# Attention maxima in two-bank PSUM tiles, one VectorE reduction per step, blocks of two row pairs

## The chip, the core and the metric

The kernel runs on one core of a Trainium2 chip. The metric is the device time of one launch in microseconds (us); of several runs the median is taken. A core has TensorE (PE in the profile; its weight loads are PEld), VectorE (DVE), ScalarE (ACT), GpSimd (POOL) and SyncE (SP), which issues most DMAs. PSUM holds eight banks of 512 fp32 values for each of 128 partitions; a matmul writes into one bank.

## The reference, cut to what matters

One block of a transformer with a conditioned layer norm: attention with 32 heads of 16 over 2048 tokens of 512 features, and after it a token-mixing and a channel MLP. The change touches attention alone:

```
q, k, v = split(h @ wqkv)                        # 32 heads of 16, S = 2048
scores  = einsum("bhqd,bhkd->bhqk", q, k) * 16**-0.5
p       = softmax(scores, axis=-1)
x       = x + ga * ((p @ v) @ wo)
```

The kernel takes the maximum of each row of scores before the exponential, so it computes the scores twice: once with queries on the partitions, for the row maxima, and later with keys on the partitions, for the exponentials that go into the product with v.

## The kernel before

**Units and steps.** Attention is cut into 64 units: 4 chunks of 512 queries (`ci`), in each 16 pairs of heads (`pr`). The two heads of a pair, `j` = 0 and 1, lie on partitions 0 to 63 and 64 to 127 of the tiles `qtl` (queries) and `kst` (keys). A unit has 16 steps, one for each tile of 128 keys, 1024 steps in all (`NS`). A step `s` has two *row pairs*, one for each `j`. A row pair (`row_pair`) issues two matmuls of 512 columns that lie on different halves of TensorE's rows: one of the scores of step `s` (`score_part`, L1012, tile `sc`) and one of the scores of step `s + 24` (`LEAD`) for the maxima (`max_part`, L996, tile `mb`). Where the score is that of `j`, the maximum is that of `1 - j`, and the matmul on rows 0 to 63 is issued first.

**Who empties the banks.** ScalarE turns each score bank into exponentials (L1008, `pt<-sc`, 128x512); VectorE reduces each maxima bank to one column (L992, `mx<-mb`, 128x512 to 128x1). When a unit's 32 reductions are through, `max_fin` reduces the columns to 8 maxima (L1042), two ScalarE copies and one GpSimd operation split them into two parts, and DMAs put them into spare rows of `qtl`, so that the score matmul subtracts them.

**The second half of a probability.** An exponential is kept as two 16-bit halves. The low halves of a step (128x1024) must be converted once (`p_low`). GpSimd does it (L1061); where the planner holds GpSimd to be over 200 ns further behind than ScalarE (`LACT`), ScalarE does it (L156, the line of a helper).

**Column parts.** `pv_part` issues four matmuls of 32 columns at a time into the single `pv` bank (L1086 for the high halves of a step, L1083 for the low halves of two). A pair of steps has three such parts. At a unit's end ScalarE copies `pv` out (`ac`, L1103), TensorE transposes the copy with eight matmuls (`ot`, L1113), ScalarE copies these (L1120), VectorE takes reciprocals (L1128) and GpSimd multiplies.

**Banks.** `pv` has one bank. The other seven are slots of one bank each (`NSM`, class `Slots`), and whoever asks next, a score, a maxima tile or `ot`, takes the slot that comes free first.

**The order.** All instructions are emitted by a planner on the host (`Sched`), which keeps an expected time for each engine (605 ns for a reduction, 480 for an exponential, 232 for a row pair, 240 for a column part) and so fixes each engine's order; on the chip semaphores decide when each starts. The main loop goes by *blocks*: `GRP` = 3 row pairs, that is one step and a half, and then the column parts of steps that lie `LAG` = 2 blocks back. The first 256 steps share TensorE with leftover projections; steps 256 to 993 have attention, nearly alone; in the last 30 (`T0S`) the next stage begins.

```
def room(self, n=1):
    if self.slots:
        return self.open is None and len(self.owner) < self.most and min(self.slots.t) <= self.T["P"]
blocks = [list(range(i, min(i + GRP, 2 * NS))) for i in range(-2 * LEAD, 2 * NS, GRP)]
```

Of the kernel before, what the change touches and what calls it, by code (L numbers as in the profile page):

```python
# [8 lines left out]
F32 = mybir.dt.float32  # L9
# [5 lines left out]
AF = mybir.ActivationFunctionType  # L15
OP = mybir.AluOpType
AX = mybir.AxisListType
# [4 lines left out]
P = 128  # L22
# [31 lines left out]
LENDS = -4  # L54
LATE = 1e9
GRP = 3
CPER = 1
LACT = 200.0
PRE = 1
# [52 lines left out]
class Sched:  # L112
# [163 lines left out]
    def room(self, n=1):  # L276

        if self.slots:
            return self.open is None and len(self.owner) < self.most and min(self.slots.t) <= self.T["P"]
        for x in [x for x in self.back if x[1] <= self.T["P"]]:  # L280
            self.back.remove(x)
            self.avail.append(x[0])
        return len(self.avail) >= n
# [21 lines left out]
class Slots:  # L305


    def __init__(self, n):
        self.t = [0.0] * n

    def take(self):
        return min(range(len(self.t)), key=lambda i: self.t[i])

    def late(self):
        return sum(t == LATE for t in self.t)
# [15 lines left out]
def kernel(ctx, tc, A_x, A_wqkv, A_wo, B_w1, B_w2, B_w3, B_w4, c, w_mod, out):  # L331
# [622 lines left out]
    psd["d"], psd["s"] = ap_, True  # L954

    unit_tiles(at, 1, pool, pool)
    qst, vst, mxs = {}, {}, {}
# [15 lines left out]
    sm = Slots(NSM)  # L973
    e_exp, e_hi, e_low, v_free, acs = {}, {}, {}, [0.0], []

    def bank(nm):
        x = sm.take()
        return x, ap_.tile([P, CH], F32, name=nm, tag=f"s{x}", bufs=1)

    def max_part(m, j):  # L980

        u, i = divmod(m, 16)
        c, g = divmod(i, 4)
        if u not in mxs:
            mxs[u] = at.tile([P, 2, 4, NC], F32, name="mx", tag="mx", bufs=2)
        x, b = bank("mb")
        ready, sm.t[x] = sm.t[x], LATE
        r = slice(64 * j, 64 * j + 62)
        lhs = qst[u][r, (g // 2) * 256:(g // 2 + 1) * 256].rearrange("p (n l) -> p l n", l=2)[:, g % 2]

        def after(e):
            end = sch.crit("D", 605, e + PX, lambda: dve.reduce_max(mxs[u][:, j, g, c:c + 1], b, axis=AX.X))  # L992
            sm.t[x] = end + XP["D"]
            if (c, g, j) == (NC - 1, 3, 0):
                max_fin(u)
        return ready, lambda: te.matmul(b, lhs, kst[u % 3][r, c * CH:(c + 1) * CH], start=True, stop=True), after  # L996

    def score_part(s, j):

        u, kt = divmod(s, NKT)  # L1000
        if j == 0:
            pt[s] = at.tile([P, 2, CH], I32, name="pt", tag="pt", bufs=NPT)
        x, b = bank("sc")
        ready, sm.t[x] = sm.t[x], LATE
        r = slice(64 * j, 64 * j + 64)

        def after(e):
            ea = sch.crit("A", 480, e + PX, lambda: act.activation(pt[s][:, j], b, AF.Exp))  # L1008
            sm.t[x] = ea + XP["A"]
            if j:  # L1010
                e_exp[s] = e_hi[s] = ea
        return ready, lambda: te.matmul(b, kst[u % 3][r, kt * P:(kt + 1) * P], qst[u][r], start=True, stop=True), after  # L1012

    def row_pair(s, j):

        parts = []
        if 0 <= s < NS:
            parts.append((j, score_part(s, j)))
        if s + LEAD < NS:
            parts.append((1 - j, max_part(s + LEAD, 1 - j)))  # L1020
        parts = [x for _, x in sorted(parts, key=lambda x: x[0])]

        def mms():
            for _, mm, _ in parts:
                mm()
        e = sch.put("P", CROW, max(x[0] for x in parts), mms)
        return [partial(x[2], e) for x in parts]

    def max_fin(u):
        mf = at.tile([P, 8], F32, name="mf", tag="mf", bufs=2)  # L1030
        nm = at.tile([P, 2, 8], F32R, name="nm", tag="nm", bufs=2)
        mx = mxs.pop(u)

        def shift_rows():
            for j in range(2):
                for i in range(2):
                    r = 64 * j + 62 + i
                    for h in range(2):
                        sch.dma(dma.dma_start,
                                qst[u][r:r + 1, h * 256:(h + 1) * 256].bitcast(F32).rearrange("o (p l) -> o p l", l=2),  # L1040
                                nm[:, i, 4 * j + 2 * h:4 * j + 2 * h + 2].bitcast(F32))
        sch.chain(("D", 85, lambda: dve.reduce_max(mf.rearrange("p (j g) -> p j g", j=2), mx, axis=AX.X)),  # L1042
                  ("A", 100, lambda: act.activation(mf, mf, AF.Copy, scale=-1.0, bias=PEXP)),
                  ("A", 100, lambda: act.activation(nm[:, 0], mf, AF.Copy)),
                  ("G", 250, lambda: pool.tensor_tensor(nm[:, 1], mf, nm[:, 0], op=OP.subtract)),
                  (None, 0, shift_rows), mark(("shift", u)), prio=0, ready=sch.T["D"])
# [549 lines left out]

    blocks = [list(range(i, min(i + GRP, 2 * NS))) for i in range(-2 * LEAD, 2 * NS, GRP)]
    pvs = [x for s in range(0, NS, 2) for x in ((s, 0), (s + 1, 0), (s, 1))]  # L1600
    due = 0.0
    for k, blk in enumerate(blocks + [[]] * (LAG + CPER)):
        if blk and blk[0] <= LENDS <= blk[-1]:
            sch.most = MOST
        for x in blk:
            if x % 2 == 0:
                if x == blk[0]:
                    before(x // 2)
                if x >= 0 and x % 32 == 0:
                    drain(("shift", x // 32))  # L1610
        if acs:
            ac_copy()
        row = [divmod(x, 2) for x in blk if x < 2 * NS]
        s0 = row[0][0] if row else 0
        col = []
        if k >= LAG and (k % CPER == 0 or not blk):

            x = (blocks[min(k - LAG, len(blocks) - 1)] or [-1])[-1]
# [3 lines left out]
        need = sum((s >= 0) + (s + LEAD < NS) for s, _ in row)  # L1622
        sch.flush(need)
        banks = sorted(sm.t)
        n = 0
        for s, i in row:
            n += (s >= 0) + (s + LEAD < NS)

            start = max(start, banks[n - 1 + 2 * (s < 0)] - t)
            t += CROW  # L1630
        t += CMID
        for s, i in col:
            start = max(start, pv_ready(s, i) - t)
            t += CCOL
        sch.gap(start)
        sch.flush(need)
        sch.T["P"] = max(sch.T["P"], start) + CIN
        low = sorted(e_exp)
        for s, i in row:
            for fn in row_pair(s, i):  # L1640
                fn()
        for x in blk[1:]:
            if x % 2 == 0:
                before(x // 2)
        for s in low:
            p_low(s)
        sch.T["P"] += CMID
        for s, i in col:
            pv_part(s, i)
        sch.T["P"] += COUT  # L1650
        for e in "ADG":
            sch.misc(e, max(sch.T["P"], sch.T[e]) + TOLE[e])
        if s0 < 0:
            sch.fill(LEADB / 2 * len(blk))
        elif sch.gens:
            late = s0 >= NS - T0S
            due += RATE3 if late else RATE if s0 < NS // NC else RATE2
            if due >= (BURST3 if late else BURST if s0 < NS // NC else BURST2):
                sch.fill(due)
                due = 0.0  # L1660
        if 2 * (NS // NC) - 1 in blk:
            for key in (("v", 1), ("kq", 3), ("q", 0), ("q", 1), "pieces"):
                drain(key)
            qpx.close()
            sch.gapmin = GAPMIN2
            ot = o0x.enter_context(tc.tile_pool(name="ot", bufs=1, side="right"))
            for ci in range(1, NC):
                oh[ci] = ot
                osb[ci] = ot.tile([P, TPC, D], F32, name=f"osb{ci}", tag=f"osb{ci}", bufs=1)
            fa = o0x.enter_context(tc.tile_pool(name="fa", bufs=1, side="right"))  # L1670
            big = {"A4": fa.tile([P, 4 * KT * 2 * P], F32R, name="A")}
            big["A"] = big["A4"]
        if blk and blk[0] <= 2 * (NS - T0L) <= blk[-1]:
            sch.add(tail_loads())
        if blk and blk[0] <= 2 * (NS - T0S) <= blk[-1]:
            sch.add(tail(0))
    if acs:
# [3 lines left out]
    sch.most = 0  # L1681
    while sch.owner:
        sch.step()
    apx.close()
    sch.banks(8)
    with ExitStack() as ex:
# [44 lines left out]
```

## Time and profile before

| what | value |
|---|---|
| median of 3 runs | 2022.87 us (2017.93 to 2027.44) |
| profiled execution | span of 2019.7 us; the runs' median is 3.2 us above |
| busy over the span | PE 96%, DVE 82%, ACT 75%, POOL 78% |
| granted TensorE clock | 0.992 mean |

How to read it: the span is from the first to the last instruction of one profiled execution. A busy share is an average over stages with different limits; the page therefore shows each engine in 40 slices of the span, and a view by windows gives the busy time of each engine in one stretch. The groups by line give count, busy time and the mean duration of one instruction. A duration reaches from an instruction's start to the acknowledgement of its last write, while the next instruction of VectorE or ScalarE may start some 80 ns before that; so the distance between neighbours is read from a row of the timeline that merges many of them. "Idle before" is time in which the engine waited, with the instruction that released it. Matmuls on different row or column groups of TensorE run side by side, so a step of TensorE is read from the starts of neighbouring groups, not from its busy share.

### The profile page before, as it was taken

Reading aid. Unit: us, or ns where it says so; the run is one execution under the profiler, and the core shown is the slowest. Engines: PE = TensorE matmul, PEld = TensorE weight load, DVE = VectorE, ACT = ScalarE, POOL = GpSimd, SP = SyncE. Lnnn points to the kernel's source line nnn. Section 1 sums busy time; section 2 is a strip of 40 time slices with the busy share of each in tenths; the row PEclk is TensorE's granted clock in tenths of the full one; section 3 lists DMA queues with packets and bytes.
Section 4 is the critical chain, followed back from the end, with each engine's and each line's share of the span. In section 5 each row is a group of like instructions: output and inputs, shape, how many; then the busy total and the mean of one; then the engine's idle time right before and its main releaser. Section 6 shows DMA issues by size and latency. Waiting matters only on the chain.

```text
span 2019.7 us, 41655 instructions
## 1 busy us (share of the span) xinstructions
PE 1934.4 (96%) x14456; PEld 1162.1 (58%) x14456; DVE 1656.3 (82%) x2979; ACT 1510.2 (75%) x3085; POOL 1571.9 (78%) x1488
## 2 busy tenths in 40 slices
PE   7999999999999999999999999999998999999999
PEld 5755545454444444444444444444455878898998
DVE  6398888879999999999999999999975886556443
ACT  6438987768999999999999999999985544344443
POOL 6349988879999999999999999999996554435222
PEclk9989999999999999999999999999999999999999
DMA  8777675445343434444443435354414676553541
GB/s 295 233 204 192 151 187 155 135 130 124 86 92 87 91 88 83 96 82 97 81 98 75 104 72 107 72 136 126 99 46 158 230 261 265 226 200 116 201 153 68
DMA packets 185508, 278.01 MB, mean 138 GB/s; under 512 B 117104, under 2 KB 127856, under 8 KB 169008
## 3 DMA queue, kind: packets, MB, share of 16 engines
q1 hardware_dynamic: 181792, 267.20, 49.1%
q10 hardware_dynamic: 2304, 4.20, 0.6%
q0 software_dynamic: 1200, 3.93, 0.5%
q8 instruction: 115, 1.88, 0.4%
q14 instruction: 97, 0.79, 0.1%
HBM read 211.81 MB, written 62.91 MB: 136 GB/s over the span
## 4 chain that ended last, share of the span: by engine, by line
PE 61%; DVE 16%; ACT 9%; issue 6%; POOL 4%; DMA 3%; SPq 0%; ACTq 0%; POOLq 0%; DVEq 0%
PE mb L996 13%; DVE mx L992 12%; PE pv L1086 9%; PE sc L1012 8%; ACT pt L1008 7%; PE w L363 5%; PE w L359 5%; PE w L361 5%; PE pv L1083 4%; PE ot L1113 3%; POOL pt L1061 2%; PE xT L1247 1%; POOL trs L1356 1%; PE v L359 1%; DMA wr<-Ws 1%
## 5 line engine op out<-in xcount | busy, mean ns | idle before, releaser
L1061 POOL TENSOR_SCALAR pt<-pt 128x1024 f16<-128x1024 uint16 x953 | 1248.3, 1367 | 79.9 <-ACT pt L1008 76.7
L992 DVE TENSOR_REDUCE mx<-mb 128x1 f32<-128x512 f32 x2048 | 1250.0, 681 | 72.7 <-PE mb L996 63.5
L1008 ACT ACTIVATE pt<-sc 128x512 int32<-128x512 f32 x2048 | 1060.9, 614 | 123.5 <-PE mb L996 97.1
L996 PE MATMUL mb<-kst,qtl 62*128 62x512 f32 x2048 | 781.1, 461 | 20.5 <-ACT pt L1008 10.0
L1012 PE MATMUL sc<-qtl,kst 64*128 64x512 f32 x2048 | 739.3, 449 | 4.6 <-DVE mx L992 1.8
L996 PEld LDWEIGHTS mb<-kst,qtl 62*128 62x128 f32 x2048 | 358.9, 193 | 233.7 <-ACT pt L1008 160.4
L1012 PEld LDWEIGHTS sc<-qtl,kst 64*128 64x128 f32 x2048 | 336.6, 185 | 185.4 <-DVE mx L992 118.7
L1086 PE MATMUL pv<-pt,vst 128*32 128x512 f16 x4096 | 384.8, 397 | 20.6 <-ACT ac L1103 20.6
L1460 POOL TENSOR_TENSOR g<-sq,g 128x256 fp32r<-128x256 f32 (+1 forms) x124 | 96.8, 785 | 188.9 <-ACT g L1459 176.6
L1083 PE MATMUL pv<-pt,vst 128*32 128x512 f16 (+1 forms) x2048 | 220.8, 389 | 2.5 <-POOL pt L1061 2.4
L1086 PEld LDWEIGHTS <-vst 128*32 128x32 bf16 x4096 | 91.8, 93 | 227.2 <-issue 208.8
L361 PE MATMUL w<-A,wr 128*128 128x256 f32 (+1 forms) x520 | 153.4, 295 | 0.3 <-DVE A L349 0.3
L359 PE MATMUL w<-A,wr 128*128 128x256 f32 (+1 forms) x520 | 153.2, 295 | 0.3 <-ACT A L353 0.3
L363 PE MATMUL w<-A,wr 128*128 128x256 f32 (+1 forms) x520 | 153.1, 294 | 0.0
L1456 ACT ACTIVATE sq<-w 128x256 f32<-128x256 f32 (+1 forms) x130 | 52.1, 401 | 127.0 <-PE w L363 117.5
L363 PE MATMUL w<-wr,g 128*128 128x512 f32 x270 | 106.5, 394 | 3.1 <-POOL g L1460 3.1
L359 PE MATMUL w<-wr,g 128*128 128x512 f32 x270 | 106.9, 396 | 1.8 <-DMA wr<-Ws 1.8
L361 PE MATMUL w<-wr,g 128*128 128x512 f32 x270 | 106.1, 393 | 0.0
L1438 DVE SCALAR_TENSOR_TENSOR sq<-sq,w 128x256 f32<-128x256 f32 (+1 forms) x130 | 58.1, 449 | 56.5 <-ACT sq L1458 56.3
L359 PEld LDWEIGHTS w<-A,wr 128*128 128x128 f32 x520 | 98.7, 190 | 1.7 <-ACT A L353 0.5
L361 PEld LDWEIGHTS w<-A,wr 128*128 128x128 f32 x520 | 98.7, 190 | 1.6 <-DVE A L349 0.5
L363 PEld LDWEIGHTS w<-A,wr 128*128 128x128 f32 x520 | 98.6, 190 | 0.5 <-issue 0.5
(156 smaller groups left out, 2131.6 us busy)
## 6 DMA issues: line engine op xcount, KB each, us to landing
wr<-Ws SPq DMA_DIRECT2D x66, 1024.0 KB, 5.2
vst<-Vs SPq DMA_DIRECT2D x64, 768.0 KB, 5.7
kst<-Ks SPq DMA_DIRECT2D x126, 384.0 KB, 6.1
Ws<-wr SPq DMA_DIRECT2D x14, 1024.0 KB, 5.0
qtl<-Qs SPq DMA_DIRECT2D x128, 96.0 KB, 4.3
Vs<-vt SPq DMA_DIRECT2D x32, 384.0 KB, 4.2
Ks<-qk SPq DMA_DIRECT2D x16, 512.0 KB, 3.8
Qs<-qk SPq DMA_DIRECT2D x16, 512.0 KB, 3.0
```

Of the source, the lines that this page charges most:

```text
L359: te.matmul(o, lh, rh, start=first, stop=False)
L361: te.matmul(o, lh, rl, start=False, stop=False)
L363: te.matmul(o, ll, rh, start=False, stop=last)
L992: end = sch.crit("D", 605, e + PX, lambda: dve.reduce_max(mxs[u][:, j, g, c:c + 1], b, axis=AX.X))
L996: return ready, lambda: te.matmul(b, lhs, kst[u % 3][r, c * CH:(c + 1) * CH], start=True, stop=True), after
L1008: ea = sch.crit("A", 480, e + PX, lambda: act.activation(pt[s][:, j], b, AF.Exp))
L1012: return ready, lambda: te.matmul(b, kst[u % 3][r, kt * P:(kt + 1) * P], qst[u][r], start=True, stop=True), after
L1061: e_low[s] = XP["G"] + sch.crit("G", 1345, ready, lambda: pool.tensor_scalar(o, i, 0.5, 1.0, op0=OP.mult, op1=OP.mult))
L1083: te.matmul(acc[r:r + n, :], v[:, kt + i, c:c + n].bitcast(F16), pt[s + i].bitcast(F16)[:, j, 0::2], start=False, stop=kt == NKT - 2, skip ...
L1086: te.matmul(acc[r:r + 32, :], v[:, kt, r:r + 32], pt[s].bitcast(F16)[:, j, 1::2], start=kt == 0, stop=False, skip_group_check=True)
L1113: te.matmul(b[:, t * n:(t + 1) * n], ac[:, t * P:(t + 1) * P], smat.rearrange("p j d -> p (j d)"), start=True, stop=True)
L1460: ("G", cG(n), lambda: pool.tensor_tensor(lo, sq, hi, op=OP.subtract)), (None, 0, end), bank=b)
```

## The change

From step 256 to step 993 the seven slots are two tiles of two banks and three tiles of one bank. Both maxima matmuls of a step (`j` = 1 and then `j` = 0) write into the halves of one two-bank tile, and one VectorE instruction reduces both halves, 128x1024 to 128x2, after the second. Scores and `ot` use the three single banks. A block has two row pairs there (`GRP2`), one step, and column parts follow three blocks behind (`LAG2`). In a row pair the score's matmul is now issued first, everywhere. At the two borders `layout` waits until no miscellaneous tile is held and opens a new pool of PSUM tiles. The maxima are stored in another order, which `max_fin` reads with a stride.

```
-        self.t = [0.0] * n
+        self.sizes, self.t = sizes, [0.0] * len(sizes)
...
+GRP2, LAG2 = 2, 3
+CMAX2 = 1138
+    def layout(sizes):
+        while sch.owner:
+            sch.step()
+        bkx.close()
+        psd["d"] = bkx.enter_context(tc.tile_pool(name="bk", bufs=1, space=PSUM))
+        sm.sizes, sm.t = sizes, [sch.T["P"]] * len(sizes)
...
     def max_part(m, j):
+        two = 2 in sm.sizes
+        if two and j == 0:
+            x, ready, b = half.pop(m)
+        else:
+            x, ready, b = bank("mb", 1 + two)
+            half[m] = x, ready, b
+        k = 1 - j if two else 0
...
-            end = sch.crit("D", 605, e + PX, lambda: dve.reduce_max(mxs[u][:, j, g, c:c + 1], b, axis=AX.X))
+            if not two:
+                end = sch.crit("D", 605, e + PX, lambda: dve.reduce_max(mxs[u][:, i, 1 - j:2 - j], b, axis=AX.X))
+            elif j == 0:
+                end = sch.crit("D", CMAX2, e + PX, lambda: dve.reduce_max(mxs[u][:, i], b, axis=AX.X))
+            else:
+                return
...
-            parts.append((j, score_part(s, j)))
+            parts.append(score_part(s, j))
-            parts.append((1 - j, max_part(s + LEAD, 1 - j)))
-        parts = [x for _, x in sorted(parts, key=lambda x: x[0])]
+            parts.append(max_part(s + LEAD, 1 - j))
...
-    blocks = [list(range(i, min(i + GRP, 2 * NS))) for i in range(-2 * LEAD, 2 * NS, GRP)]
+    blocks = [list(range(i, min(i + n, b))) for a, b, n in ((-2 * LEAD, 2 * (NS // NC), GRP), (2 * (NS // NC), 2 * (NS - T0S), GRP2),
+                                                            (2 * (NS - T0S), 2 * NS, GRP)) for i in range(a, b, n)]
...
+            layout([2, 2, 1, 1, 1])
...
+        if blk and blk[-1] == 2 * (NS - T0S) - 1:
+            layout([1] * NSM)
```

`room`, which lets `ot` take a slot, and the planner's estimate of when a block may start now look at the earliest single bank and the earliest two-bank tile.

More of the change, by code (lines that the diff above doesn't have):

```diff
@@ L278, in room @@
         if self.slots:
-            return self.open is None and len(self.owner) < self.most and min(self.slots.t) <= self.T["P"]
+            return self.open is None and len(self.owner) < self.most and self.slots.t[self.slots.take()] <= self.T["P"]
         for x in [x for x in self.back if x[1] <= self.T["P"]]:
@@ L305, with __init__, take @@
 class Slots:
-    def __init__(self, n):
-        self.t = [0.0] * n
-    def take(self):
-        return min(range(len(self.t)), key=lambda i: self.t[i])
+    def __init__(self, sizes):
+        self.sizes, self.t = sizes, [0.0] * len(sizes)
+    def take(self, size=1):
+        return min((i for i, z in enumerate(self.sizes) if z == size), key=lambda i: self.t[i])
     def late(self):
@@ L953 @@
     ap_ = apx.enter_context(tc.tile_pool(name="ap", bufs=1, space=PSUM))
-    psd["d"], psd["s"] = ap_, True
+    bkx = ExitStack()
+    psd["s"] = True
     unit_tiles(at, 1, pool, pool)
@@ L971, in load_v, with bank @@
         sch.dma(dma.dma_start, vst[u], Vs[units[u][1]])
-    sm = Slots(NSM)
-    e_exp, e_hi, e_low, v_free, acs = {}, {}, {}, [0.0], []
-    def bank(nm):
-        x = sm.take()
-        return x, ap_.tile([P, CH], F32, name=nm, tag=f"s{x}", bufs=1)
+    sm = Slots([])
+    def layout(sizes):
[5 more added lines that the diff above has]
+    layout([1] * NSM)
+    e_exp, e_hi, e_low, v_free, acs = {}, {}, {}, [0.0], []
+    def bank(nm, size=1):
+        x = sm.take(size)
+        ready, sm.t[x] = sm.t[x], LATE
+        return x, ready, psd["d"].tile([P, size, CH], F32, name=nm, tag=f"s{x}", bufs=1)
+    half = {}
     def max_part(m, j):
@@ L984, in max_part @@
         if u not in mxs:
-            mxs[u] = at.tile([P, 2, 4, NC], F32, name="mx", tag="mx", bufs=2)
-        x, b = bank("mb")
-        ready, sm.t[x] = sm.t[x], LATE
+            mxs[u] = at.tile([P, 16, 2], F32, name="mx", tag="mx", bufs=2)
+        two = 2 in sm.sizes
[5 more added lines that the diff above has]
+        k = 1 - j if two else 0
         r = slice(64 * j, 64 * j + 62)
@@ L995, in after @@
                 max_fin(u)
-        return ready, lambda: te.matmul(b, lhs, kst[u % 3][r, c * CH:(c + 1) * CH], start=True, stop=True), after
+        return ready, lambda: te.matmul(b[:, k], lhs, kst[u % 3][r, c * CH:(c + 1) * CH], start=True, stop=True), after
     def score_part(s, j):
@@ L1002, in score_part @@
             pt[s] = at.tile([P, 2, CH], I32, name="pt", tag="pt", bufs=NPT)
-        x, b = bank("sc")
-        ready, sm.t[x] = sm.t[x], LATE
+        x, ready, b = bank("sc")
         r = slice(64 * j, 64 * j + 64)
         def after(e):
-            ea = sch.crit("A", 480, e + PX, lambda: act.activation(pt[s][:, j], b, AF.Exp))
+            ea = sch.crit("A", 480, e + PX, lambda: act.activation(pt[s][:, j], b[:, 0], AF.Exp))
             sm.t[x] = ea + XP["A"]
@@ L1011, in after @@
                 e_exp[s] = e_hi[s] = ea
-        return ready, lambda: te.matmul(b, kst[u % 3][r, kt * P:(kt + 1) * P], qst[u][r], start=True, stop=True), after
+        return ready, lambda: te.matmul(b[:, 0], kst[u % 3][r, kt * P:(kt + 1) * P], qst[u][r], start=True, stop=True), after
     def row_pair(s, j):
@@ L1616 @@
         if k >= LAG and (k % CPER == 0 or not blk):
-            x = (blocks[min(k - LAG, len(blocks) - 1)] or [-1])[-1]
+            x = (blocks[min(k - (LAG2 if 2 in sm.sizes else LAG), len(blocks) - 1)] or [-1])[-1]
             while pvs and 2 * (pvs[0][0] + pvs[0][1]) < x and not (col and pvs[0][0] % NKT == 0 and not pvs[0][1]):
@@ L1621 @@
         t, start = CIN, 0.0
-        need = sum((s >= 0) + (s + LEAD < NS) for s, _ in row)
+        two = 2 in sm.sizes
+        need = 4 if two else sum((s >= 0) + (s + LEAD < NS) for s, _ in row)
         sch.flush(need)
@@ L1625 @@
         n = 0
-        for s, i in row:
+        for s, i in row[:2 if two else GRP]:
             n += (s >= 0) + (s + LEAD < NS)
-            start = max(start, banks[n - 1 + 2 * (s < 0)] - t)
+            start = max(start, (max(sm.t[sm.take()], sm.t[sm.take(2)]) if two else banks[n - 1 + 2 * (s < 0)]) - t)
             t += CROW
+        t += CROW * len(row[2:]) if two else 0.0
         t += CMID
@@ L1674 @@
             sch.add(tail_loads())
+        if blk and blk[-1] == 2 * (NS - T0S) - 1:
+            layout([1] * NSM)
         if blk and blk[0] <= 2 * (NS - T0S) <= blk[-1]:
@@ L1683 @@
         sch.step()
+    bkx.close()
     apx.close()
```

5 lines of the change are left out of this document (3 added, 2 removed).

## The prediction

> **What bounds the kernel now.** I began with the page's busy shares and slices, to find where the changed steps lie.
>
> ```profile
> PE 1934.4 (96%) x14456; PEld 1162.1 (58%) x14456; DVE 1656.3 (82%) x2979; ACT 1510.2 (75%) x3085; POOL 1571.9 (78%) x1488
> ...
> DVE  6398888879999999999999999999975886556443
> ```
>
> VectorE's row stands at 9 from the eleventh to the twenty-eighth slice: the middle of attention, where the change works. Its average of 82% hides that. Next, that stretch in the view by windows, and its groups by line:
>
> ```profile
> 540.00:1470.00 930.00, 899.96 (x7662) 426.56 (x7662) 891.24 (x1551) 859.82 (x1704) 891.76 (x760) 1.00 0.44 94
> ```
>
> ```profile
> L992 DVE TENSOR_REDUCE mx<-mb 128x1 f32<-128x512 f32 x1459 | 887.1, 681 | 32.4 <-PE mb L996 26.2 <-PE sc L1012 3.1
> L1061 POOL TENSOR_SCALAR pt<-pt 128x1024 f16<-128x1024 uint16 x669 | 871.0, 1363 | 32.9 <-ACT pt L1008 30.3
> L1008 ACT ACTIVATE pt<-sc 128x512 int32<-128x512 f32 x1459 | 752.8, 614 | 54.1 <-PE mb L996 44.6 <-PE sc L1012 2.2 <-POOL pt L1061 0.8
> ...
> L156 ACT ACTIVATE pt<-pt 128x1024 f16<-128x1024 uint16 x61 | 83.9, 1375 | 0.0
> ...
> L1113 PE MATMUL ot<-smat,ac 128*128 128x34 f32 x368 | 49.7, 280 | 0.0
> ...
> L1128 DVE RECIPROCAL rc<-sm 128x8 f32<-128x8 f32 x46 | 9.0, 195 | 6.3 <-ACT sm L1120 6.3
> L1042 DVE TENSOR_REDUCE mf<-mx 128x8 f32<-128x32 f32 x46 | 8.3, 180 | 0.1
> ```
>
> The 1459 reductions, two to a step, are 729.5 steps in 930 us: 1.275 us a step. In the window's row the columns are PE, PEld, DVE, ACT, POOL: VectorE is busy 95.8% of it, POOL 95.9%, ScalarE 92.5%. Before its reductions VectorE idled 32.4 us, 3.5%: it bounds the stretch and is fed nearly without a break, but two others stand close behind. The waits say who feeds it:
>
> ```profile
> PEld mb L996 <- ACT pt L1008: 134.1, 394, 0.8
> PEld sc L1012 <- DVE mx L992: 98.4, 254, 0.5
> ...
> DVE mx L992 <- PE mb L996: 26.2, 55, 0.8
> ...
> PE pv L1086 <- ACT ac L1103: 18.7, 16, 1.2
> ```
>
> TensorE's weight loads wait for ScalarE or VectorE to free a slot. It waits crosswise, a maxima tile for an exponential and a score for a reduction, because all share seven slots. TensorE therefore has time to spare, and the common slots keep VectorE supplied when ScalarE is late.
>
> **Part 1: one reduction for two.** Removed: 738 reductions (steps 256 to 993). What is left of each pair grows to 1024 elements. No row shows a two-bank instruction; these bound it:
>
> ```profile
> 979.64 18.62 DVE L992 TENSOR_REDUCE mx<-mb 128x1 f32<-128x512 f32 x31
> ```
>
> ```profile
> L1560 DVE TENSOR_TENSOR x<-x,w 128x512 f32<-128x512 f32 x73 | 48.9, 684 | 59.1 <-PE w L363 58.8
> ...
> L1457 DVE SCALAR_TENSOR_TENSOR sq<-sq,w 128x256 f32<-128x256 f32 x102 | 42.7, 419 | 32.0 <-ACT sq L1456 27.6
> ```
>
> Back to back a reduction takes (18.62 - 0.08)/31 = 0.598 us (the 0.08 is the last one's tail). Between 256 and 512 elements a VectorE instruction grows by 684 - 419 = 265 ns, so by 0.530 for 512 more. Estimate for two banks: 0.598 + 0.530 = 1.128 us against 2 x 0.598 = 1.196; it saves 0.068 a step, 50 us of VectorE in all. Its ends are no saving (each bank pays the whole price) and the ratio of the elements alone, 2 x 0.530 = 1.06. I take 1.128, since both rows are of this stream of fp32. With the unit's small instructions, (9.0 + 8.3)/729.5 = 0.024, VectorE's floor falls from 1.220 to 1.152 a step.
>
> The Trainium skill ("Perfetto Trace Analysis", Optimizing Scalar/DVE Operations) puts the fixed part of a VectorE instruction on PSUM at about 125 ns and recommends larger operations on a saturated engine. By that figure the engine would save 0.125 a step, 92 us in all; the rows here bear out about half, and the sum goes by the rows.
>
> **Part 2: the other floors.** A gain stops at the next engine. ScalarE and POOL share the low halves:
>
> ```profile
> 981.11 4.73 ACT L1008 ACTIVATE pt<-sc 128x512 int32<-128x512 f32 x9
> ...
> 987.84 1.37 ACT L156 ACTIVATE pt<-pt 128x1024 f16<-128x1024 uint16 x1
> 989.03 4.51 ACT L1008 ACTIVATE pt<-sc 128x512 int32<-128x512 f32 x9
> ```
>
> A low half holds ScalarE from 987.84 to 989.03: 1.19 us. Without its 61 of them ScalarE is busy (859.82 - 61 x 1.19)/729.5 = 1.079 a step. POOL takes 871.0/669 = 1.302 for one and has (891.76 - 871.0)/729.5 = 0.028 beside. If ScalarE does a share f: 1.079 + 1.19 f = 0.028 + 1.302 (1 - f), so f = 0.101 and both are full at 1.199 a step. Today f is 61/729.5 = 0.084.
>
> **Part 3: shorter blocks.** TensorE's own pace, in a stretch where it hardly waits:
>
> ```profile
> 816.72 0.41 PE L1086 MATMUL pv<-pt,vst 128*32 128x512 f16 x4
> 816.96 0.40 PE L1083 MATMUL pv<-pt,vst 128*32 128x512 f16 x4
> 817.18 0.40 PE L1086 MATMUL pv<-pt,vst 128*32 128x512 f16 x4
> 817.51 0.49 PE L1012 MATMUL sc<-qtl,kst 64*128 64x512 f32 x1
> 817.52 0.72 PE L996 MATMUL mb<-kst,qtl 62*128 62x512 f32 x2
> 817.87 0.63 PE L1012 MATMUL sc<-qtl,kst 64*128 64x512 f32 x2
> 818.10 0.40 PE L996 MATMUL mb<-kst,qtl 62*128 62x512 f32 x1
> 818.43 0.41 PE L1086 MATMUL pv<-pt,vst 128*32 128x512 f16 x4
> ```
>
> From start to start: column part to column part 0.23; to the first row pair 0.33; that to the second 0.36; to the third 0.23; to the next columns 0.33. A block of three pairs has 2.25 column parts on average: 0.33 + 0.36 + 0.23 + 0.33 + 1.25 x 0.23 = 1.54 for a step and a half, 1.025 a step. A block of two pairs has 1 and 2 in turn: 0.33 + 0.36 + 0.33 + 0.5 x 0.23 = 1.135 a step. So the change adds 0.11 a step of switching to TensorE, 81 us, today under cover of its waits (134.1 + 98.4 us in the window, 0.32 a step). With the transposes, 49.7/46 = 1.08 a unit, 0.068 a step, TensorE's floor rises from 1.093 to 1.203. That is now the highest of the floors (1.152, 1.199, 1.203); the cover is gone, and each wait TensorE still has counts in full.
>
> **Part 4: the tiles as a wait.** A maxima tile turns thus: 1.21 for the reduction to its reported end (1.128 + 0.08), a hand-over, the second row pair's 0.23, its matmul's 0.50, a hand-over.
>
> ```profile
> 799.71 3.00 DVE mx L992 x5
> 802.71 0.04 issue
> 802.75 0.50 PE mb L996
> ```
>
> The chain of waits puts a hand-over at 0.04 and this matmul at 0.50. The turn is 2.02, and two tiles give 2 x 1.128 = 2.26: 0.24 to spare. What TensorE is later than that, VectorE idles. Behind a maxima matmul that waits stand, on TensorE, the step's second score, its second maximum and its column parts; ScalarE and VectorE both wait for these.
>
> Three score banks turn faster (0.49 + 0.04 + 0.61 + 0.04 = 1.18, for one and a half steps), except when ScalarE takes a low half. Let step k's first score start at 0: its exponentials run from 0.53 and from 1.05 to 1.56 ((4.73 - 0.09)/9 = 0.515 each), the low half to 2.75, the next step's first exponential to 3.36 with its tail, so its bank is free at 3.40. At 1.2 a step the second score of step k + 2 wants it at 2.40 + 0.36 = 2.76. TensorE stands for about 0.65 (0.7 where the weights load late as well), with the maximum queued behind. At f = 0.084 that is 0.059 a step. A low half that falls near a transpose costs nothing, as ScalarE gets no scores for 1.08 there; that is two steps in sixteen. Ends: nothing (today a late ScalarE costs VectorE next to nothing: 26.2 us of waits on TensorE's maxima from all causes) and 0.071 at f = 0.101. I take 0.059 x 7/8 = 0.052. The 18.7 us that TensorE waits for `ac` come of the same late ScalarE and aren't added.
>
> **Part 5: edits near nothing.** Column parts stay three steps behind (two blocks of 1.5, three of one). The score now goes first in every pair; the two matmuls of a pair start 0.01 apart (817.51 and 817.52), so their order is worth no more. The strided L1042 reads the same 32 values; doubled, it would cost an engine with slack 0.18 a unit. The DMAs of the shifts stay, eight a unit. Each of the two changes of layout lets the banks drain: two or three reductions of 0.598 that nothing overlaps, 1 to 2 us, 3 together.
>
> **The sum.** TensorE's 1.203 + 0.052 = 1.255 a step against 1.275: 0.020 x 738 = 15 us, less 3: 12 us. From the span of 2019.7 that is 2008; the runs' median lies 3.2 above the span: 2011.
>
> **The rivals.**
>
> *Stalls hidden (0.2).* The planner has GpSimd catch up and puts transposes where ScalarE is late. For it: VectorE waits for TensorE's maxima only 55 times today, 0.8 us at most, though 61 low halves fall to ScalarE. Against it: that is with seven shared slots, and the scores will have three. The floor would be 1.203 at best, 53 - 3 = 50 us; halfway to the forecast, 1.229, it is 34 - 3 = 31: about 1992.
>
> *Two tiles starve VectorE, slower (0.27).* Blocks have one or two column parts: 1.02 and 1.25 us, the long one 0.12 over VectorE's 1.128. The 0.24 to spare covers that while TensorE is ahead. After a transpose (1.08) or a stall (0.65) it isn't, and then a short block waits for its tile and wins nothing back: 0.12 in two steps, 0.06 a step, over half the steps 0.03 to all of them 0.06. From 1.255, 0.035 gives 1.29: +11 + 3; 0.06 gives 1.315: +30 + 3. I price it at 1.30: +18 + 3, 2044. It decides against the change once such waits pass 0.016 a step (what is left of 0.020 after the 3 us). The Trainium skill's same section says that where Vector isn't saturated but makes bubbles on other engines, breaking instructions up may finish sooner: this change does the opposite. For that rival speaks the rank of the floors, TensorE over VectorE; against it, that today's idling of VectorE is 3.5%.
>
> *The instruction saves nothing (0.08).* If two banks cost 1.196, VectorE's floor stays at 1.220 and its slack against TensorE's 1.255 is halved; with half of the 0.035 above I get 1.272 to 1.28: 0 to +4, +3: 2027.
>
> **How the numbers follow.** About 0.5%, 10 us, is what a measurement of this kernel tells from no change. The forecast (0.45) spreads with its stalls between 0.035 and 0.071 a step: from a gain of 24 us to a loss of 2, some 55% of it over a gain of 10. Faster: 0.25 + 0.2 = 0.45. Same: 0.20, and the mild parts of the second and third rival, 0.04 + 0.05: 0.29. Slower: 0.26. The range leaves out a tenth at each end: below, the rest of the first rival under 1987 (1.224 a step); above, the second beyond 1.301, 2045.
>
> **What would show it.** Right: two-bank reductions at 1.13 apart and 1.2 long; the stretch at 1.255 a step, 926 us for 738; VectorE's idling up to some 8%, released by PE; TensorE's waits for reductions nearly gone and those for exponentials about 0.05 a step, in lumps of 0.6 behind each ScalarE low half. Wrong: reductions at 1.19 (third rival); short blocks that wait for VectorE after each transpose and over 1.275 a step (second); waits under 0.02 a step (first). A stretch outside steps 256 to 993 that moves by over 3 us would show that the new order in a pair, which I cost at nothing, has a price.

## The result, and the profile after

The changed kernel takes 2568.46 us (median of 4 runs, 2566.64 to 2572.53), the kernel before, run beside it, 2020.9: a ratio of 1.2712, 95% interval 1.2685 to 1.2738. It is 548 us slower, where the forecast said 12 us faster and the range ended at 2045.

The slices of the page after, as before, show the middle of attention:

```profile
PE   8999999976666666666666666666676889999999
...
DVE  5688888965555555555555555555565658865543
...
PEclk9999999988787888888888888888888889999999
```

VectorE has fallen from 9 to 5, but TensorE from 9 to 6 as well, and the granted clock dips all through the stretch. No engine is full: all wait for something else. The first score of step 256 and of step 994 start 1472.7 us apart in this trace, against 941.1 before, 1.996 us a step against 1.275. The page's groups name the wait (count, busy time and mean, then idle before it and its releasers):

```profile
L1086 POOL TENSOR_SCALAR pt<-pt 128x1024 f16<-128x1024 uint16 x920 | 1212.8, 1360 | 635.1 <-ACT pt L1033 631.8
L1033 ACT ACTIVATE pt<-sc 128x512 int32<-128x512 f32 x2048 | 1090.2, 603 | 600.7 <-PE mb L1022 576.6
L1016 DVE TENSOR_REDUCE mx<-mb 128x2 f32<-128x1024 f32 x738 | 868.7, 1219 | 576.8 <-PE mb L1022 492.5
L1037 PE MATMUL sc<-qtl,kst 64*128 64x512 f32 x2048 | 831.5, 485 | 470.2 <-DMA qtl<-nm 451.4
```

POOL waits for ScalarE, ScalarE and VectorE wait for TensorE, and TensorE waits for a DMA: `qtl<-nm`, the shift by which a unit's maxima come into the score matmul. Before, that releaser stood in no row. One unit's start in the changed kernel, TensorE by the timeline:

```profile
990.48 0.39 PE L1037 MATMUL sc<-qtl,kst 64*128 64x512 f32 x1
990.79 0.41 PE L1111 MATMUL pv<-pt,vst 128*32 128x512 f16 x4
1001.35 0.76 PE L1037 MATMUL sc<-qtl,kst 64*128 64x512 f32 x1 [10.15 <-DMA qtl<-nm]
```

The shift's data were ready well before: POOL's last operation on them (`nm`), in the same stretch, ended at 983.85.

```profile
983.65 0.20 POOL L1070 TENSOR_TENSOR nm<-mf,nm 128x8 fp32r<-128x8 f32 x1
```

SyncE's queue shows where they stood. First the changed kernel, then the one before, in its like place:

```profile
990.65 0.30 SPq L137 DMA_DIRECT2D qtl<-Qs  x1
991.02 0.41 SPq L137 DMA_DIRECT2D kst<-Ks  x1
991.53 0.35 SPq L137 DMA_DIRECT2D qtl<-Qs  x1
991.93 0.42 SPq L137 DMA_DIRECT2D kst<-Ks  x1
992.45 8.50 SPq L137 DMA_DIRECT2D qtl<-nm  x8
```

```profile
981.23 5.81 SPq L135 DMA_DIRECT2D qtl<-nm  x8
987.14 0.53 SPq L135 DMA_DIRECT2D qtl<-Qs  x1
987.72 0.42 SPq L135 DMA_DIRECT2D kst<-Ks  x1
988.23 0.37 SPq L135 DMA_DIRECT2D qtl<-Qs  x1
988.64 0.42 SPq L135 DMA_DIRECT2D kst<-Ks  x1
```

Before, the eight shift DMAs stand ahead of the four loads for the unit after the next; after, behind them. The loads overwrite the tiles of the unit that is just ending, so the first one must wait for that unit's last score, which starts at 990.48. The queue keeps its order: the shift, ready at 983.85, goes out at 992.45, its eight DMAs take 8.50 us to issue instead of 5.81, and TensorE, whose next score needs them, stands for 10.15 us. Most of that is no longer the late issue, which comes only 1.25 us after TensorE stopped (991.20). It is the landing: the four loads carry 960 KB, the shift's small packets start only at 996.82, with the loads' last large one at 996.89, and the first shift DMA lands 8.2 us after its issue. In the kernel before, it lands 1.9 us after. The changed kernel itself has two units of the other kind: for units 57 and 62 the shift goes out 9.0 and 8.1 us before the unit's first score, ahead of any load, and TensorE doesn't wait for it.

The clock adds to the loss. Windows of the changed kernel (PE, PEld, DVE, ACT, POOL, granted clock, DMA share, GB/s):

```profile
994.00:998.00 4.00, 0.00 (x0) 0.00 (x0) 0.00 (x0) 0.00 (x0) 0.00 (x0) 0.60 1.02 122
998.00:1001.30 3.30, 0.00 (x0) 0.00 (x0) 0.00 (x0) 0.00 (x0) 0.00 (x0) 0.50 0.01 0
1001.30:1004.00 2.70, 2.31 (x12) 0.78 (x12) 0.68 (x1) 1.19 (x2) 0.00 (x0) 0.50 0.03 0
...
1008.00:1009.00 1.00, 1.00 (x12) 0.60 (x8) 0.41 (x1) 0.79 (x2) 0.98 (x1) 0.77 0.00 0
1009.00:1010.00 1.00, 1.00 (x12) 0.50 (x12) 0.98 (x1) 1.00 (x3) 0.38 (x1) 1.00 0.86 258
```

With TensorE idle the clock goes to half, and it is full again only 7 us after work resumed. The three steps from 1001.35 to 1008.02 take 6.67 us there. On average over 45 units a unit's first three steps take 6.37 us in this kernel and 4.43 in the kernel of the first experiment below, which doesn't wait. So each unit that waits pays about 10 us of waiting and some 2 of slow steps; 45 units do.

### The profile page after: what moved, and what is told of

The parts are those of the page before. It is cut to its first block, busy times and chain, and to the rows that moved or that the text cites. A ratio compares the mean times of both kernels' runs of the same rounds, so it can differ in the third digit from the quotient of the medians.

```text
span 2567.3 us, 40747 instructions
## 1 busy us (share of the span) xinstructions
PE 2042.7 (80%) x14456; PEld 1154.8 (45%) x14456; DVE 1637.4 (64%) x2241; ACT 1580.5 (62%) x3118; POOL 1538.0 (60%) x1455
## 4 chain that ended last, share of the span: by engine, by line
PE 60%; DMA 19%; ACT 6%; DVE 5%; issue 4%; POOL 3%; SPq 2%; ACTq 0%; POOLq 0%; DVEq 0%
PE sc L1037 18%; DMA kst<-Ks 14%; PE pv L1111 11%; PE mb L1022 7%; PE pv L1108 4%; PE w L365 4%; PE w L361 4%; ACT pt L1033 4%; PE w L363 4%; DMA qtl<-nm 3%; SPq L137 2%; DVE mx L1014 2%; PE ot L1138 1%; POOL pt L1086 1%; POOL trs L1381 1%
## 5 line engine op out<-in xcount | busy, mean ns | idle before, releaser
L1086 POOL TENSOR_SCALAR pt<-pt 128x1024 f16<-128x1024 uint16 x920 | 1212.8, 1360 | 635.1 <-ACT pt L1033 631.8
L1033 ACT ACTIVATE pt<-sc 128x512 int32<-128x512 f32 x2048 | 1090.2, 603 | 600.7 <-PE mb L1022 576.6
L1016 DVE TENSOR_REDUCE mx<-mb 128x2 f32<-128x1024 f32 x738 | 868.7, 1219 | 576.8 <-PE mb L1022 492.5
L1037 PE MATMUL sc<-qtl,kst 64*128 64x512 f32 x2048 | 831.5, 485 | 470.2 <-DMA qtl<-nm 451.4
L1022 PE MATMUL mb<-kst,qtl 62*128 62x512 f32 x2048 | 845.1, 495 | 4.5 <-DVE vr L771 1.6
L1037 PEld LDWEIGHTS sc<-qtl,kst 64*128 64x128 f32 x2048 | 367.4, 202 | 873.4 <-issue 555.1
L1111 PE MATMUL pv<-pt,vst 128*32 128x512 f16 x4096 | 434.5, 423 | 8.1 <-ACT ac L1128 7.6
L1014 DVE TENSOR_REDUCE mx<-mb 128x1 f32<-128x512 f32 x572 | 352.0, 680 | 39.0 <-PE mb L1022 38.3
L158 ACT ACTIVATE pt<-pt 128x1024 f16<-128x1024 uint16 x104 | 140.9, 1355 | 0.0
L361 PEld LDWEIGHTS w<-A,wr 128*128 128x128 f32 x520 | 99.8, 192 | 4.7 <-DVE sq L1463 3.5
L363 PEld LDWEIGHTS w<-A,wr 128*128 128x128 f32 x520 | 99.7, 192 | 1.5 <-DVE A L351 0.4
```

The source lines that it names most:

```text
L361: te.matmul(o, lh, rh, start=first, stop=False)
L363: te.matmul(o, lh, rl, start=False, stop=False)
L1016: end = sch.crit("D", CMAX2, e + PX, lambda: dve.reduce_max(mxs[u][:, i], b, axis=AX.X))
L1022: return ready, lambda: te.matmul(b[:, k], lhs, kst[u % 3][r, c * CH:(c + 1) * CH], start=True, stop=True), after
L1037: return ready, lambda: te.matmul(b[:, 0], kst[u % 3][r, kt * P:(kt + 1) * P], qst[u][r], start=True, stop=True), after
L1086: e_low[s] = XP["G"] + sch.crit("G", 1345, ready, lambda: pool.tensor_scalar(o, i, 0.5, 1.0, op0=OP.mult, op1=OP.mult))
```

## The experiments

**Theory.** The *queue theory*: the added time is the shift stuck behind the loads in SyncE's queue, and it comes of the planner. It emits a due shift only when it looks at its list of due work, which it does while it fills a gap of over 500 ns or runs other generators. With blocks of one step there is hardly such a gap, so the shift is emitted at the latest moment, at its own unit's start. There the loads come first in the code where the unit begins a block: with blocks of two pairs every unit does, with blocks of three one in three. The rival, the forecast's second, is the *tile theory*: two tiles and three banks starve VectorE and ScalarE.

**The shift put first.** The changed kernel with two statements swapped:

```
                 if x % 2 == 0:
-                if x == blk[0]:
-                    before(x // 2)
                 if x >= 0 and x % 32 == 0:
                     drain(("shift", x // 32))
+                if x == blk[0]:
+                    before(x // 2)
```

> The changed kernel, with two planner statements swapped: at a unit's start the eight DMAs of the unit's shift go into SyncE's queue before the four loads for the unit after the next, not behind them. Queue theory (the added time is the shift stuck behind loads that wait for the last score of the unit before): TensorE's waits of 10 us a unit vanish, 46 units give back 500 us and more, and what is left is the change as the forecast worked it out: 1.24 to 1.30 us a step, 1995 to 2045 us. Tile theory (two maxima tiles and three score banks starve VectorE and ScalarE): the wait only changes its name; over 2300 us.

Measured: 2048.72 us, 1.0133 of before (1.0117 to 1.0149). The swap gives back 520 of the 548 us. SyncE's queue in this run:

```profile
1007.28 4.99 SPq L137 DMA_DIRECT2D qtl<-nm  x8
1014.30 0.31 SPq L137 DMA_DIRECT2D qtl<-Qs  x1
1014.65 0.42 SPq L137 DMA_DIRECT2D kst<-Ks  x1
```

The rest, 28 us of loss, is the change itself.

**The same defect in the old kernel.** Seven one-bank slots and blocks of three pairs as they were; for the 15 units of the stretch that begin a block, the shift is kept until the loads are out:

```
+                  (None, 0, partial(held.__setitem__, u, shift_rows) if u in range(18, 63, 3) else shift_rows),
...
                 if x >= 0 and x % 32 == 0:
                     drain(("shift", x // 32))
+                    if x // 32 in held:
+                        held.pop(x // 32)()
```

> The kernel before, seven one-bank slots and blocks of three pairs as they are; only for the 15 units of the middle stretch whose start falls on a block's start the shift is held back until it stands behind the loads in SyncE's queue. Queue theory: about 10 us for each of the 15, some 150 to 180 us in all, 2170 to 2200 us. Tile theory: nothing, 2021 us, since the banks are untouched.

Measured: 2194.48 us (ratio 1.0856, 1.0838 to 1.0875), 174 us more than before, 11.6 for each of the 15. Its waits (us in all, times, longest):

```profile
PE sc L1012 <- DMA qtl<-nm: 131.0, 15, 9.1
```

Fifteen waits of 8.7 us in the mean, 131 us in all; the other 43 us come behind these waits. No bank was touched.

**Short blocks alone.** The kernel before with blocks of two pairs in the stretch and column parts three blocks behind:

```
+    blocks = [list(range(i, min(i + n, b))) for a, b, n in ((-2 * LEAD, 2 * (NS // NC), GRP), (2 * (NS // NC), 2 * (NS - T0S), 2),
+                                                            (2 * (NS - T0S), 2 * NS, GRP)) for i in range(a, b, n)]
```

> The kernel before, with blocks of two pairs from step 256 to 993 and column parts three blocks behind; seven one-bank slots and single reductions stay. Queue theory: every unit now starts at a block's start, so the loads stand ahead of the shift for 46 units: 10 us each and a colder clock after it, 2480 to 2570 us. Tile theory: at most the price of more switching that the covers leave, under 2080 us.

Measured: 2592.24 us (1.2825, 1.2803 to 1.2846): with neither a two-bank tile nor a joined reduction, the whole loss and somewhat more. The wait is the same:

```profile
PE sc L1012 <- DMA qtl<-nm: 435.8, 45, 10.5
```

**Short blocks, shift first.** The same with the swap of the first experiment.

> As the run with short blocks and single slots, with the shift put before the loads. Queue theory: back near the kernel before; VectorE's floor of 1.220 a step is unchanged and TensorE's is 1.203, so 1.27 to 1.30 a step, 2015 to 2045 us. Tile theory says nothing of this one; if short blocks themselves cost the time it stays above 2400 us.

Measured: 2045.25 us (1.0127, 1.0112 to 1.0142). So of the 28 us that the mended change loses, seven slots and single reductions lose 25 too: they are the price of short blocks, and the two-bank tiles bring nothing on top.

**The planner looks after each block.** The changed kernel with its statements as they were, and

```
+        if NS // NC <= s0 < NS - T0S:
+            sch.marks()
```

> The changed kernel with its order at a unit's start unchanged; the planner only looks after each block of the middle stretch whether a shift is due, and so emits it some seven steps before the unit starts. Queue theory, with the cause in the planner (blocks without gaps never look): the same as the run with the shift first, 2049 us within 5. If the statement order at the unit's start were the whole cause by itself: still 2568.

Measured: 2056.09 us (1.0181, 1.0159 to 1.0202), 512 us less than the changed kernel; 7 more than with the swap. That is one unit: the shift of unit 16 is due before step 256, where this edit doesn't look yet, and the first score of step 256 starts 8.9 us later in this trace than in the swapped kernel's. So either cure is enough: it takes both a planner that doesn't look and an order that puts the loads first.

**The planner looks, in the kernel before.** The same two lines in the old kernel.

> The kernel before, with the planner looking for a due shift after each block of the middle stretch. Queue theory: its shifts already stand ahead of the loads, so nothing is won: 2021 us within 8. If late shifts had already cost it time: 10 us or more less.

Measured: 2020.34 us (1.0002, 0.9992 to 1.0012). Nothing was hidden there.

**What the joined reduction is worth.** The swapped kernel with each tile reduced by two instructions:

```
-                end = sch.crit("D", CMAX2, e + PX, lambda: dve.reduce_max(mxs[u][:, i], b, axis=AX.X))
+                end = sch.crit("D", CMAX2, e + PX, lambda: [dve.reduce_max(mxs[u][:, i, h:h + 1], b[:, h], axis=AX.X) for h in range(2)])
```

> The run with the shift first, same order and same tiles, but each two-bank tile is reduced by two instructions of 512 elements, both after the second matmul. VectorE gets 738 x 0.068 = 50 us more work. Share theory: ScalarE bounds, VectorE had 8% of idle time, so the step (1.30) still holds VectorE's 1.220: 2049 to 2060. Theory that the joined reduction carries the step: 40 to 50 us more, 2090 to 2100.

Measured: 2049.19 us (1.0140, 1.0124 to 1.0155), the same as 2048.72. The joined reduction does what it says: in the swapped kernel's timeline six in a row take 6.89 us, (6.89 - 0.09)/6 = 1.133 each.

```profile
989.02 6.89 DVE L1016 TENSOR_REDUCE mx<-mb 128x2 f32<-128x1024 f32 x6
```

But nobody waits for the time it saves.

**Fewer low halves for ScalarE.** In the swapped kernel ScalarE is busy 95.8% of the stretch and has 92 low halves there, where the forecast's balance gave 75. Three planner costs are set to the durations of the trace (`CLOW` is 1150). The same was done to the kernel with short blocks and single slots. Both have the shift first; the edit of the first:

```
-            ea = sch.crit("A", 480, e + PX, lambda: act.activation(pt[s][:, j], b[:, 0], AF.Exp))
+            ea = sch.crit("A", 515 if 2 in sm.sizes else 480, e + PX, lambda: act.activation(pt[s][:, j], b[:, 0], AF.Exp))
...
-                e_low[s] = XP["A"] + sch.crit("A", CLOW, ready, partial(act.activation, o[:, c], i[:, c], AF.Copy, scale=0.5))
+                e_low[s] = XP["A"] + sch.crit("A", 1190 if 2 in sm.sizes else CLOW, ready, partial(act.activation, o[:, c], i[:, c], AF.Copy, scale=0.5))
...
-            e_low[s] = XP["G"] + sch.crit("G", 1345, ready, lambda: pool.tensor_scalar(
+            e_low[s] = XP["G"] + sch.crit("G", 1305 if 2 in sm.sizes else 1345, ready, lambda: pool.tensor_scalar(
```

> The run with the shift first, with three planner costs of the middle stretch set to what the trace shows (exponential 515 for 480, low half on ScalarE 1190 for 1150, on GpSimd 1305 for 1345), so that ScalarE is given 86 low halves for 104. Share theory (ScalarE bounds the mended kernel, 95.8% busy, since the planner gives it 12.4% of the low halves where 10.1% would balance): 18 x 1.19 = 21 us less, about 2028. Bank theory (three score banks and two tiles bound it, whoever does the low halves): within 8 us of 2049.

> Short blocks, seven one-bank slots, shift first, and the same three planner costs: ScalarE is given 103 low halves for 127. Share theory: with ScalarE's share down VectorE's 1.220 a step is the next floor, so some 10 to 20 us less than 2045: 2025 to 2035, about 1.28 a step, and behind the two-bank kernel with the same costs by up to 10 us. Bank theory: seven shared slots must beat two tiles and three banks at the same share, so this one lies below the two-bank kernel with 104 low halves (2049) by 20 us or more.

Measured: 2052.06 us (1.0156, 1.0140 to 1.0171) with two-bank tiles, 2065.72 (1.0234, 1.0192 to 1.0276) with single slots. Neither gained; the second lost 20 us. The share theory falls: with 75 low halves on ScalarE for 92 the stretch is no faster; it takes 9.2 us more, and 5.2 of these are a wait for one shift (unit 57) whose eight DMAs took 10.95 us to issue. The bank theory's own expectation of the second, below 2049, fell too. Why a planner with truer costs makes a slower order stays open.

**Low halves to VectorE.** The planner's choice is between GpSimd and VectorE there:

```
+            if g > max(sch.T["D"], ready) + LACT:
+                e_low[s] = XP["D"] + sch.crit("D", CMAX2, ready, lambda: dve.tensor_scalar(o, i, 0.5, 1.0, op0=OP.mult, op1=OP.mult))
```

> The run with the shift first, with the low halves that the planner takes from GpSimd given to VectorE (55 of them) instead of ScalarE (93 in the stretch). Stall theory (a low half on ScalarE holds three score banks, and TensorE stands 0.7 us at the next step's second pair after about half of them, 40 us in the trace): these waits vanish, 25 to 40 us less, 2010 to 2025. If ScalarE's low halves do not cause them: within 10 us of 2049. Against a full gain: VectorE gets some 1.1 us for each of 55, where it idled 57 us of 930, and GpSimd does more of them.

Measured: 2134.19 us (1.0559, 1.0533 to 1.0586), far above both expectations. The conversion takes VectorE 1.79 us, not the 1.1 I reckoned with, and TensorE now waits for maxima tiles:

```profile
L1022 PE MATMUL mb<-kst,qtl 62*128 62x512 f32 x1476 | 564.5, 481 | 61.9 <-DVE mx L1016 61.8
...
L1081 DVE TENSOR_SCALAR pt<-pt 128x1024 f16<-128x1024 uint16 x55 | 98.7, 1794 | 0.0
```

TensorE's granted clock is lower as well, 0.94 in this window where the swapped kernel has 1.00 (the two rows, this run first):

```profile
540.00:1470.00 930.00, 864.89 (x6932) 362.98 (x6932) 864.81 (x792) 739.77 (x1486) 840.86 (x693) 0.94 0.41 85
```

```profile
540.00:1470.00 930.00, 882.76 (x7538) 381.63 (x7536) 851.57 (x808) 890.96 (x1704) 841.74 (x718) 1.00 0.44 91
```

How much of the loss is the clock and how much the waits isn't shown. The run doesn't tell the stall theory true or false: a new stall took the old one's place, in the other kind of tile, and the clock changed with it.

**Longer blocks with two-bank tiles.** The swapped kernel, `GRP2, LAG2 = 4, 2`, and then `3, 2`:

> The run with the shift first, with blocks of four row pairs (two steps) in the middle stretch and column parts two blocks behind; tiles, joined reductions and statement order as there. Switch theory (the mended kernel is slower than before because short blocks raise TensorE's own step from 1.064 to 1.171 us by the trace): TensorE's own step falls to about 1.02, and even with the four scores of a block waiting on three banks (some 0.15 a step) the step falls under 1.25: 2000 to 2015 us. Bank theory (two tiles and three banks bind, whatever the blocks): four scores and two tiles in one block wait inside it, 1.30 a step or more, 2050 and up.

> The run with the shift first, with the two-bank tiles but blocks of three pairs, as the kernel before has them, and column parts two blocks behind: a tile's second half is filled in the next block in every second case. Switch theory: TensorE's own step returns to 1.064 us, and as the planner then gives ScalarE only 11 low halves, GpSimd's floor of 0.028 + 1.302 x 0.99 = 1.317 a step bounds it: about 1.33, 2065 us. Bank theory: tiles held open across a block's columns starve VectorE as well: 1.36 or more, 2085 and up. Under 2020 would say that short blocks alone cost the time.

Measured: 2091.6 us (1.0347, 1.0324 to 1.0369) and 2076.77 (1.0272, 1.0252 to 1.0291); 1.363 and 1.345 us a step over the stretch. For TensorE's *own step* I took from the traces, for each kind of neighbours (a pair after columns, columns after a pair, and so on), the 5th percentile of the distance between their starts times their number; what is over is waiting:

| kernel | own step | waiting | step |
|---|---|---|---|
| before, blocks of 3 pairs, 7 slots | 1.064 | 0.209 | 1.273 |
| shift first, blocks of 2, two-bank | 1.171 | 0.124 | 1.296 |
| short blocks, shift first, 7 slots | 1.172 | 0.127 | 1.300 |
| blocks of 4, two-bank | 1.03 to 1.16 | 0.20 to 0.33 | 1.364 |
| blocks of 3, two-bank | 1.066 | 0.277 | 1.344 |

(650 steps from the middle of each stretch.) In the kernel with four pairs the split is rough: the fourth pair of a block never starts less than 0.487 us behind the third, since there are three score banks for four scores, and whether that counts as own step or as waiting depends on which distances are taken together. The switch theory's first half holds from two pairs to three: the own step falls from 1.171 to 1.066. Its forecast for four doesn't: the step came out at 1.363, not under 1.25. The waits there are for score banks:

```profile
PEld sc L1037 <- ACT pt L1033: 291.9, 648, 1.3
...
PEld mb L1022 <- DVE mx L1016: 54.4, 253, 0.3
```

With three pairs the planner gave ScalarE 11 low halves, all of them outside the stretch. GpSimd converts all 738 steps there and is full, 916.79 of 930 us, as the switch theory said. By part 2's figures GpSimd then needs 1.302 + 0.028 = 1.330 us a step, close to the 1.345 measured. The run's time is 12 us over that theory's 2065 and 8 under the other's 2085.

```profile
540.00:1470.00 930.00, 884.97 (x7264) 428.37 (x7256) 819.72 (x779) 767.97 (x1558) 916.79 (x779) 1.00 0.41 89
```

So in these runs the two-bank tiles did best in short blocks, and short blocks cost TensorE 0.107 a step. That longer blocks can't work with them isn't shown: with three pairs GpSimd was full, and another share of low halves wasn't tried. No version beat the kernel before.

## Why the prediction was wrong, step by step

**The step that failed is in part 5**, "edits near nothing": "The DMAs of the shifts stay, eight a unit." They stay in number, but not in place. I counted what the change issues and didn't ask, for SyncE's queue, what now stands ahead of what. Two things were in view. The planner's due work is emitted only in gaps, and my part 3 had just argued that TensorE's gaps would go. And at a unit's start the loads come before the shift where the unit begins a block, and blocks of two pairs always begin there (32 pairs a unit). TensorE waited 450.8 us for these DMAs in 45 units: 10.0 just before step 256 and 440.8 in the stretch, which grew by 531.6. Of the rest, 17 us are the dearer steps that stay in the swapped kernel, and some 74 the slow steps behind each wait, part of them at half clock. The cause is shown by the swap (520 us back), by the old kernel with 15 late shifts (174 us) and by short blocks alone (572 us).

**Part 1** was right: 1.133 us measured for 1.128, on 738 instructions. The trace bears out the smaller saving, 2 x 0.598 - 1.133 = 0.063, not the 0.125 that is estimated from the Trainium skill's figure ("Perfetto Trace Analysis", Optimizing Scalar/DVE Operations).

**Part 3** was right in size: TensorE's own step rose by 0.107 (forecast 0.11). Both levels lie 0.03 under my sums, mostly because I read the distance from a block's first pair to its second, 0.36, at one place; over the stretch 0.34 is usual.

**Part 4's stall** exists as described, somewhat longer than the 0.65 to 0.7 forecast. In the trace of the swapped kernel a low half holds ScalarE from 1016.35 to 1017.57, and the second score of a later step waits, with the maximum behind it:

```profile
1016.35 1.36 ACT L158 ACTIVATE pt<-pt 128x1024 f16<-128x1024 uint16 x1
1017.57 2.06 ACT L1033 ACTIVATE pt<-sc 128x512 int32<-128x512 f32 x4
```

```profile
1017.05 0.50 PE L1037 MATMUL sc<-qtl,kst 64*128 64x512 f32 x1
1017.05 0.50 PE L1022 MATMUL mb<-kst,qtl 62*128 62x512 f32 x1
1018.20 0.50 PE L1037 MATMUL sc<-qtl,kst 64*128 64x512 f32 x1 [0.65 <-ACT pt L1033]
```

The second pair should start 0.34 behind the first, at 1017.39; it starts at 1018.20, 0.81 late (the row's 0.65 counts from the end of the matmul before). The median of such stalls is 0.80. They follow 47 of the 92 low halves, and all late second pairs of the stretch together are 40 us, 0.054 a step, where I took 0.052. That the sum agrees so well is partly luck: ScalarE had 92 low halves and not 62, but only half of them stalled TensorE.

What I missed is the other 0.07 of TensorE's waits: the forecast let it run at its own step between the stalls, and it doesn't. By the table it still waits 0.124 in all; what makes the 0.07 isn't shown. That is why the mended change gives 1.2985 a step over the stretch and not 1.255, a loss of (1.2985 - 1.275) x 738 = 17 us. Another 2 to 10 us come behind step 993: from the first score of step 994 to the end the kernel before takes 540 us in its trace and every other trace here 543 to 550. The run with late shifts and the old kernel with the planner looking, both with the old blocks and banks, take 546 and 547, so this part is not tied to the short blocks or the tiles; it stays open.

**The rivals.** The first is out, since the stalls are in the trace, and the third, since the joined reduction takes 1.133 and not 1.196. The second named the sign, not the mechanism. The mended kernel, at 2048.72, lies near its price (2044), but VectorE is not starved by its tiles there: TensorE's waits are for exponentials (206.5 us), and in the first seven rows of its waits TensorE waits for no reduction.

```profile
PEld sc L1037 <- ACT pt L1033: 206.5, 417, 1.4
...
DVE mx L1016 <- PE mb L1022: 42.0, 61, 0.8
```

**The order in a pair** cost nothing that can be seen, as forecast. Where no late shift stands before it, the first score of step 256 starts at 534.5 to 538.2 us in the five traces with the old order, and at 537.1 to 539.5 in the six with the new.

## What to carry to other kernels

A change that takes away an engine's gaps also takes away whatever the schedule did in them: list the work that is emitted "when there is time", and ask where it goes when there is none. For each queue that keeps its order, write down what stands ahead of what before and after, above all small late transfers that someone needs at once against early loads that wait for a buffer, and count the time that the loads' data take. And a saving on one engine has to be paid for in the same units: here 0.06 us a step on VectorE was bought with 0.107 on TensorE, whose waiting had hidden it only in part.

## What the runs showed of the hardware that I had not expected

- A waiting DMA at the head of SyncE's queue held eight small ones behind it for 8.6 us (ready 983.85, out 992.45). Behind the loads these also went out slower, 8.50 us for eight, than ahead of them, 4.99: the sixth, seventh and eighth each went out only when an earlier load had landed. The first landed 8.2 us after its issue, in the kernel before 1.9.
- The granted clock fell to 0.50 at 994.81, 3.6 us after TensorE had stopped, and came back to 1.00 at 1008.47, 7.1 us after it had resumed. The Trainium skill ("TensorE: Matmul & The Clock Gate", Part 1) gives about 3.4 us of sustained work for that; here it took twice as long, in a stretch in which TensorE still waited between groups.
- A VectorE conversion of 128x1024 from 16-bit integers to 16-bit floats with a stride of two elements took 1.79 us, longer than GpSimd's 1.39 for the same in that run.
- The two-bank reduction saved 0.063 us of two single ones, at 1.133.
